# Grouped-query decode attention on one core: fewer instructions on VectorE and GpSimd

## The chip, the core and the metric

The kernel runs on one core of a Trainium2 chip. The metric is device time in microseconds (us) of one execution, taken as the median of ten runs. The engines are named as in the profile: PE is TensorE (matmul), PEld its weight load, DVE is VectorE, ACT is ScalarE, POOL is GpSimd, SP is SyncE, which here only issues transfers. Sixteen DMA engines move data between HBM and the core's memory (SBUF).

## The reference

One attention block with a key/value cache: 32 sequences of 4 new tokens, 32 query heads on 4 key/value heads of width 128, 2048 cached positions.

```python
B, Sq, D = 32, 4, 1024
Hq, Hkv, Sk, Dh = 32, 4, 2048, 128
...
q = (x @ wq).reshape(B, Sq, Hq, Dh)            # per head
scores = jnp.einsum("bhqd,bhkd->bhqk", q, k) * (Dh ** -0.5)
p = _softmax(scores, axis=-1)
o = jnp.einsum("bhqk,bhkd->bhqd", p, v)
return o.transpose(0, 2, 1, 3).reshape(B, Sq, Hq * Dh) @ wo
```

All arrays are bfloat16. K and V are 2 MB each per sequence, so 64 tiles of 2 MB, wq and wo are 8 MB each.

## The kernel before, in words

The program is written by hand, engine by engine. `_Program` collects each engine's operations in the order in which they are recorded and turns their dependences into semaphore waits. There is no scheduler: the order in the source is the order on the engine. On GpSimd every operation also waits for the one before it (`last_pool`).

**Transfers.** SP issues all loads in one fixed list: x, four pieces of wq, the first three K tiles, then V and K tiles in turn (line 189 on), then wo in eleven pieces (line 216 on). A tile of 2 MB has 128 rows of 16 KB, one per partition. The big buffer has eight slots: four for V, three for K, and one that GpSimd uses for masked probabilities. A K load waits until K of three sequences before was turned (`kt`, line 205), a V load until the product with V of four sequences before is done (`pv`, line 203). The wo pieces go into the slots of the last three K tiles and of V 28.

**One step** (line 436 on) handles sequence i up to its softmax, and sequence i-3 (LAG) with V:

- `kt(i+1)` (line 317): VectorE turns K in blocks of 32x32 as 32-bit words, in four chunks of 128x1024. Two chunks stand ahead of the max of step i, two behind it.
- `qd(i+1)` (line 307): GpSimd copies q of one sequence into a block-diagonal buffer, four copies of 32x64, one for each key/value head. A token `t_qd` is given to PE.
- `pe_qk(i)` (line 325): 16 matmuls write 128 x 2048 scores. PE takes `t_kt`, `t_qd` and `t_exp`.
- `softmax_max` (line 344): a max over the scores on VectorE, and a second small operation that multiplies it by -scale.
- `softmax_exp` (line 349): ScalarE computes exp(scale * s + bias) and the row sums.
- `pe_sum`, `recip` (lines 361, 365): a matmul with one column gathers the sums, VectorE takes their reciprocal.
- `pt(i)` (line 356): VectorE turns the probabilities; two buffers.
- `pd(i-1)` (line 371): GpSimd spreads them into a block-diagonal buffer, four copies of 32x1024; a token `t_pd` is given to PE. For the last two sequences VectorE does some of them.
- `pe_pv(i-3)` (line 381): 64 matmuls with V. `o_evac` (line 393): ScalarE scales by the reciprocal and writes o over that sequence's q.
- `o_turn` (line 399): VectorE turns o for the output projection, four sequences at a time from step 22 on; the rest behind the loop (line 468).

**The end.** `oproj` (line 409) runs 64 matmuls, two for each head, in the order of the wo pieces (4, 4, 4, 4, 4, 4, 2, 2, 2, 1, 1 heads). `oproj_out` copies the result and stores it.

PE's program has a run-time loop over four steps at a time; all other engines' programs are straight code.

Of the kernel before, what the change touches and what calls it, by code (L numbers as in the profile page):

```python
# [29 lines left out]
class _Program:  # L30
# [14 lines left out]

    def op(self, engine, emit, waits=(), done=None, takes=(), gives=None):
        if engine == "pool":
            done = done or ("pool", self.count["pool"])
            waits = tuple(waits) + (self.last_pool,) * (self.last_pool is not None)
            self.last_pool = done  # L50
        if gives is not None:
            self.late[engine].append(done)
        elif done is not None:
            self.count[engine] += 1
            for d in [done] + self.late[engine]:
                assert d not in self.at, d
                self.at[d] = (engine, self.count[engine])
            self.late[engine] = []
        self.ops[engine].append((emit, tuple(waits), tuple(takes), (gives or engine, 1) if done is not None else None))
# [44 lines left out]
def bass_standalone__gqa_block_cached__sampling_kernel(  # L104
# [17 lines left out]
    TC = 16  # L122
    NCH = T // TC
    KT = D // 128
    NS = 8
# [5 lines left out]
    KS = 3  # L131
    LAG = 3
    QB = 4
    NC = D // 2
# [7 lines left out]
    with ExitStack() as es:  # L142
# [6 lines left out]
        q_sb = KT_sb[:, 1, :, :, :, :].rearrange("p t a r w -> p (t a r w)")[:, 0:Hq * Dh]  # L149
        q_sb = q_sb.rearrange("p (h a g e) -> p h a g e", h=REP, a=2, g=G)  # L150
        QT_sb = sbuf("QT_sb", [128, B, 2, REP, Sq, 2], BF16)
        oT_sb = sbuf("oT_sb", [128, Hq // 4, 2, B, Sq, 2], BF16)
        QD_sb = sbuf("QD_sb", [128, 2, 2, G, 32, 2], BF16)
# [3 lines left out]
        xT_sb = P_flat[:, D:2 * D].rearrange("p (a b) -> p a b", b=128)  # L157
        PT_sb = sbuf("PT_sb", [128, 2, T // 2, 32, 2], BF16)
        PD_sb = sbuf("PD_sb", [128, T // 2, 4, G, 8, 2], BF16)
# [4 lines left out]
        permf = sbuf("permf", [128, 128], F32)  # L164
        mx = sbuf("mx", [128, 4], F32)
        negmx = sbuf("negmx", [128, 4], F32)
# [32 lines left out]
        for kind, b in loads:  # L199
            s = slot_of(kind, b)  # L200
            waits = ["qproj"] * (b < VS) if kind == "v" else []
            if kind == "v" and b >= VS:
                waits = [("pv", b - VS)]
            if kind == "k" and b >= KS:
                waits = [("kt", b - KS, NCH - 1)]
            src = (k_cache if kind == "k" else v_cache)[b].rearrange("g (r t) d -> (g r) t d", r=R)
            p.dma("sp", lambda e, s=s, src=src: e.dma_start(big[:, s, :, :], src), waits, (kind, b), f"s_b{s}", kind == "v")
# [8 lines left out]
        for c, m in enumerate(WO):  # L216
            assert u0 // 4 == (u0 + m - 1) // 4
            kind, b = wo_for[u0 // 8]
            dst, src = wo_at(u0, m), wo_v[:, u0 // 4, u0 % 4 * D:(u0 % 4 + m) * D]
            p.dma("sp", lambda e, dst=dst, src=src: e.dma_start(dst, src),  # L220
                [("kt", b, NCH - 1) if kind == "k" else ("pv", b)], ("wo", c), f"s_wo{c}")
            u0 += m
# [46 lines left out]
        for n, j in enumerate(QJ):  # L269
            g, y = j // 2, j % 2  # L270
            dst = q_sb.rearrange("p (x y) a g e -> p x y a g e", y=2)[:, :, y, :, g, :]
            src = ps_q(j).rearrange("p (h a e) -> p h a e", h=4, a=2)
            if n % 2 == 0:
                p.op("dve", lambda e, s=src, d=dst: e.tensor_copy(d, s), [q_of(j)], ("qs", j))  # L274
            else:
                p.op("act", lambda e, s=src, d=dst: e.activation(d, s, ACT.Copy), [q_of(j)], ("qs", j))

# [29 lines left out]
        def qd(i):  # L307
            for g in range(G):
                rows = slice(32 * g, 32 * (g + 1))
                src = words(QT_sb[rows, i, :, :, :, :].rearrange("p a h s w -> p a (h s w)"))  # L310
                dst = words(QD_sb[rows, i % 2, :, g, :, :].rearrange("p a q w -> p a (q w)"))
                waits = ["qd0"] + [("qa", 3, 1)] + [("qb", 3, 1)] * (i >= QB) + ([("qk", i - 2)] if i > 1 else [])
                p.op("pool", lambda e, s=src, d=dst: e.tensor_copy(d, s), waits if g == 0 else [],  # L313
                     ("qd", i) if g == G - 1 else None)
            p.give("pool", ("qd", i), "t_qd")

        def kt(i, chunks):
            for c in chunks:
                ts = slice(TC * c, TC * (c + 1))
                src = words(big[:, slot_of("k", i), ts, :].rearrange("p t d -> p (t d)"))  # L320
                dst = words(KT_sb[:, i % 2, ts, :, :, :].rearrange("p t a r w -> p (t a r w)"))
                waits = [("k", i)] + ([("qk", i - 2)] if i > 1 else ["qt_all"] if i == 1 else [])
                p.op("dve", lambda e, s=src, d=dst: e.transpose(d, s), waits, ("kt", i, c), gives="t_kt" if c == NCH - 1 else None)  # L323

        def pe_qk(i):
            waits = [] if i else [("qs", j) for j in range(8)]
            takes = [("t_kt", 1), ("t_qd", 1)] + [("t_exp", 1)] * (i > 0)
            for a in range(2):
# [15 lines left out]
        def softmax_max(i):  # L344
            p.op("dve", lambda e: e.tensor_reduce(mx[:, i % 4:i % 4 + 1], ps_s[:, :], AX.X, ALU.max), [("qk", i)], ("mx", i))  # L345
            p.op("dve", lambda e: e.tensor_scalar(negmx[:, i % 4:i % 4 + 1], mx[:, i % 4:i % 4 + 1], -scale, None, op0=ALU.mult),  # L346
                 [("mx", i)], ("negmx", i))

        def softmax_exp(i):
            p.op("act", lambda e: e.activation(  # L350
                P_sb[:, :, :, :].rearrange("p t r w -> p t w r"), ps_s[:, :].rearrange("p (t w r) -> p t w r", w=2, r=R),
                ACT.Exp, bias=negmx[:, i % 4:i % 4 + 1], scale=scale, accum_out=ssum[:, i % 4:i % 4 + 1]),
                [("negmx", i)] + ([("pt", i - 1)] if i else ["qproj"]), ("exp", i))
            p.give("act", ("exp", i), "t_exp")

        def pt(i):
            src = words(P_flat)
            dst = words(PT_sb[:, i % 2, :, :, :].rearrange("p t q w -> p (t q w)"))
            p.op("dve", lambda e: e.transpose(dst, src), [("exp", i)] + ([("pd", i - 2, G - 1)] if i > 1 else []), ("pt", i))  # L359

        def pe_sum(i):
            p.op("pe", lambda e: e.matmul(ring[i % 4][:, 511:512], lhsT=permf[:, :], rhs=ssum[:, i % 4:i % 4 + 1], start=True, stop=True),  # L362
                 ["permf"] if i == 0 else [], ("ss", i), [("t_exp", 1)] * (i == L))

        def recip(i):
            p.op("dve", lambda e: e.reciprocal(rinv[:, i % 4:i % 4 + 1], ring[i % 4][:, 511:512]), [("ss", i)], ("rinv", i))

# [3 lines left out]
        def pd(i):  # L371
            free = ("pv", i - 2) if i > 1 else ("pd0", "pf0")[i]
            for g in range(G):
                rows = slice(32 * g, 32 * (g + 1))
                src = words(PT_sb[rows, i % 2, :, :, :].rearrange("p t (x q) w -> p (t x) (q w)", x=4))
                dst = words(pd_of(i)[rows, :, :, g, :, :].rearrange("p t x q w -> p (t x) (q w)"))
                p.op("dve" if i >= B - 2 and g < i - B + 4 else "pool", lambda e, s=src, d=dst: e.tensor_copy(d, s), [("pt", i), free], ("pd", i, g))  # L377
            if i < B - 2:
                p.give("pool", ("pd", i, G - 1), "t_pd")

        def pe_pv(i, t):
            takes, waits = [], []
            if t == 0:
                ring_of["o", i] = slot()
                takes = [("t_pd", 1)] * (i < B - 2) + [(f"s_b{slot_of('v', i)}", 16)]
                waits = [] if i < B - 2 else [("pd", i, g) for g in range(G)]
            buf = ring_of["o", i]
# [44 lines left out]
        qd(0)  # L432
        kt(0, range(NCH))
        starts = []
        idle_rhs = ident[:, :].unsqueeze(1).to_broadcast([128, IDLE // 128, 128])
        for i in range(B + LAG):
            j = i - LAG
            starts.append(len(p.ops["pe"]))
            if i < L:
                qd(i + 1)  # L440
                kt(i + 1, (0, 1))
            if i < B:
# [4 lines left out]
            if i < B:  # L447
                pe_idle(20 if i < LAG else 5, ring[j % 4][:, 0:IDLE], idle_rhs, [("qb", 3, 1), ("qs", 3)] if i == 0 else [])
                softmax_exp(i)
            if 0 < i < B:  # L450
                recip(i - 1)
            if i < L:
                kt(i + 1, (2, 3))
            if 21 < i and 4 * (i - 22) + 4 <= i - LAG:
                o_turn(4 * (i - 22), 4)
            if i < B:
# [9 lines left out]
            if 0 < i <= B:  # L466
                pd(i - 1)
        for b0, n in ((24, 4), (28, 2), (30, 1), (31, 1)):
            o_turn(b0, n)
# [4 lines left out]
        p.loop = starts[4:B + 1:4]  # L474
        names = list(p.ENGINES) + ["t_kt", "t_qd", "t_exp", "t_pd", "t_o"] + sorted({s for s in p.dma_count})
        sems = {n: es.enter_context(nc.semaphore(f"e_{n}" if n in p.ENGINES else n)) for n in names}
# [53 lines left out]
```

## Time and profile before

| what | value |
|---|---|
| time, median of 10 runs (lowest to highest) | 364.65 us (364.5 to 364.85) |
| the profiled execution: time, span | 364.57 us, 362.8 us |
| PE busy | 309.0 us, 85% |
| DVE busy, instructions | 279.1 us, 77%, 295 |
| ACT busy | 102.8 us, 28% |
| POOL busy, instructions | 165.4 us, 46%, 262 |
| granted PE clock | 0.995 |
| HBM read | 151.26 MB |

The span is from the first to the last instruction of the profile; 1.77 us of the execution lie around it. Idle time of an engine that is not the bound costs nothing. The groups of VectorE and GpSimd that the change touches (columns: line, engine, operation, out<-in, shapes, count | busy us, mean ns of one | idle before in us and what ended it):

```profile
L323 DVE STREAM_TRANSPOSE KT_sb<-big 128x1024 f32<-128x1024 f32 x128 | 150.1, 1212 | 7.8 <-DMA big<-in_k_cache_dram 7.8
...
L359 DVE STREAM_TRANSPOSE PT_sb<-P_sb 128x1024 f32<-128x1024 f32 x32 | 39.8, 1245 | 10.9 <-ACT P_sb L350 10.9
L366 DVE RECIPROCAL rinv<-ps_r 128x1 f32<-128x1 f32 x32 | 5.1, 158 | 0.2 <-PE ps_r L362 0.2
L346 DVE TENSOR_SCALAR negmx<-mx 128x1 f32<-128x1 f32 x32 | 4.9, 154 | 1.1
L404 DVE STREAM_TRANSPOSE oT_sb<-QT_sb 128x128 f32<-128x128 f32 x14 | 3.3, 273 | 0.0
```

GpSimd's copies are 123 of 1034 ns (`pd`) and 128 of 229 ns (`qd`).

### The profile page before, as it was taken

The page shows a single profiled execution, that of the slowest core. Times are in us where ns is not written, and L with a number is a line of the kernel's source. Part 1 is how long each engine was busy: PE and PEld are TensorE (multiplying, and loading weights), DVE is VectorE, ACT ScalarE, POOL GpSimd, SP SyncE. Part 2 cuts the span into 40 slices and gives each one's busy share as a digit, 9 for nine tenths or more (in the row PEclk, how much of TensorE's full clock was granted, in tenths as well). Part 3 has the DMA queues.
Part 4 walks back from the last instruction along what each step waited for, and adds up shares of the span by engine and source line. Part 5 has one row for each costly group of instructions (what it writes and reads, how often), then busy time and mean ns, then how long its engine had stood idle before and what let it go on. Part 6 is the DMA issues. An engine that isn't in the chain of part 4 may idle for free. (4 is left out here: it accounts for less than half of the span.)

```text
span 362.8 us, 6454 instructions
## 1 busy us (share of the span) xinstructions
PE 309.0 (85%) x3002; PEld 147.3 (41%) x2338; DVE 279.1 (77%) x295; ACT 102.8 (28%) x110; POOL 165.4 (46%) x262
## 2 busy tenths in 40 slices
PE   1988787999999999999999999888888888889796
PEld 1002000444444444444444444444433334449611
DVE  0028779999999999999999999899888888856300
ACT  1014222333333333333333333332332223333000
POOL 8002155055555555555555555444555555443000
PEclk9999989999999999999999999999999999999999
DMA  7999999999999999999999999999999999999994
GB/s 323 430 432 434 434 434 417 423 428 430 428 426 425 425 434 428 430 429 425 426 429 430 431 428 423 428 430 430 430 426 423 430 433 430 428 425 424 417 413 159
DMA packets 11822, 151.69 MB, mean 418 GB/s; under 512 B 1312, under 2 KB 1568, under 8 KB 2336
## 3 DMA queue, kind: packets, MB, share of 16 engines
q1 hardware_dynamic: 11664, 151.39, 98.4%
q8 instruction: 6, 0.10, 0.1%
q10 hardware_dynamic: 144, 0.13, 0.1%
q14 instruction: 8, 0.07, 0.0%
HBM read 151.26 MB, written 0.26 MB: 418 GB/s over the span
## 5 line engine op out<-in xcount | busy, mean ns | idle before, releaser
L323 DVE STREAM_TRANSPOSE KT_sb<-big 128x1024 f32<-128x1024 f32 x128 | 150.1, 1212 | 7.8 <-DMA big<-in_k_cache_dram 7.8
L350 ACT ACTIVATE P_sb<-ps_s,negmx 128x2048 bf16<-128x2048 f32 x32 | 82.0, 2564 | 191.2 <-DVE negmx L346 191.2
L16 PE MATMUL ps_s<-KT_sb,QD_sb 128*128 128x512 bf16 x384 | 105.0, 381 | 0.0
L377 POOL COPY PD_sb<-PT_sb 32x1024 f32<-32x1024 f32 x62 | 64.1, 1034 | 70.3 <-PE ps_r L388 45.4
L377 POOL COPY big<-PT_sb 32x1024 f32<-32x1024 f32 x61 | 63.1, 1034 | 61.2 <-PE ps_r L388 36.6
L345 DVE TENSOR_REDUCE mx<-ps_s 128x1 f32<-128x2048 f32 x32 | 73.3, 2292 | 14.3 <-PE ps_s L16 13.5
L388 PE MATMUL ps_r<-big 128*128 128x128 bf16 x1024 | 59.8, 219 | 9.7 <-PEq L85 9.5
L336 PE MATMUL ps_s<-KT_sb,QD_sb 128*128 128x512 bf16 x128 | 48.8, 381 | 21.8 <-PEq L85 21.8
L388 PE MATMUL ps_r<-big,PD_sb 128*128 128x128 bf16 x1024 | 59.8, 219 | 7.6 <-PEq L85 7.5
L388 PEld LDWEIGHTS ps_r<-big 128*128 128x128 bf16 x1024 | 58.0, 98 | 20.2 <-issue 19.7
L388 PEld LDWEIGHTS ps_r<-big,PD_sb 128*128 128x128 bf16 x1024 | 58.1, 98 | 18.4 <-issue 17.6
L336 PEld LDWEIGHTS ps_s<-KT_sb,QD_sb 128*128 128x128 bf16 x128 | 12.4, 97 | 108.4 <-issue 108.4
L359 DVE STREAM_TRANSPOSE PT_sb<-P_sb 128x1024 f32<-128x1024 f32 x32 | 39.8, 1245 | 10.9 <-ACT P_sb L350 10.9
L313 POOL COPY QD_sb<-QT_sb 32x64 f32<-32x64 f32 x128 | 29.4, 229 | 37.4 <-DVE QT_sb L292 20.3
L16 PE MATMUL ps_r<-ident 128*128 128x384 bf16 x173 | 33.3, 325 | 0.0
L362 PEld LDWEIGHTS ps_r<-ssum,permf 128*128 128x128 f32 x64 | 11.9, 187 | 24.8 <-issue 23.1
L397 ACT ACTIVATE QT_sb<-ps_r,rinv 128x128 bf16<-128x128 f32 x32 | 11.8, 367 | 24.5 <-PE ps_r L388 22.0
L274 DVE CAST KT_sb<-ps_r 128x512 bf16<-128x512 f32 x2 | 1.3, 687 | 20.1 <-PE ps_r L258 20.1
L414 PE MATMUL ps_s<-big,oT_sb 128*128 128x512 bf16 x32 | 12.2, 380 | 2.2 <-DMA big<-in_wo_dram 1.3
L423 DVE CAST P_sb<-ps_s 128x512 bf16<-128x512 f32 x1 | 0.7, 692 | 16.0 <-PE ps_s L16 16.0
L16 PE MATMUL ps_s<-big,oT_sb 128*128 128x512 bf16 x32 | 12.1, 379 | 0.0
L247 PE MATMUL ps_r<-ident 128*128 128x384 bf16 x32 | 10.3, 323 | 0.0
(42 smaller groups left out, 93.9 us busy)
## 6 DMA issues: line engine op xcount, KB each, us to landing
big<-in_k_cache_dram SPq DMA_DIRECT2D x32, 2048.0 KB, 15.4
big<-in_v_cache_dram SPq DMA_DIRECT2D x32, 2048.0 KB, 19.6
big<-in_wq_dram SPq DMA_DIRECT2D x4, 2048.0 KB, 13.9
big<-in_wo_dram SPq DMA_DIRECT2D x6, 1024.0 KB, 23.6
big<-in_wo_dram SPq DMA_DIRECT2D x3, 512.0 KB, 25.1
big<-in_wo_dram SPq DMA_DIRECT2D x2, 256.0 KB, 21.0
P_sb<-in_x_dram SPq DMA_DIRECT2D x1, 256.0 KB, 2.7
out_dram<-P_sb ACTq DMA_DIRECT2D x1, 128.0 KB, 1.8
```

What stands on the lines that cost most here:

```text
L16: return eng.add_instruction(mybir.InstMatmult(name=nc.get_next_instruction_name(), engine=eng.engine, start_tensor_calc=start, stop_tenso ...
L313: p.op("pool", lambda e, s=src, d=dst: e.tensor_copy(d, s), waits if g == 0 else [], ("qd", i) if g == G - 1 else None)
L323: p.op("dve", lambda e, s=src, d=dst: e.transpose(d, s), waits, ("kt", i, c), gives="t_kt" if c == NCH - 1 else None)
L336: mm = lambda e, a_=(out_, lhsT, rhs), f=first, l=last: e.matmul(a_[0], lhsT=a_[1], rhs=a_[2], start=f, stop=l, skip_group_check=True)
L345: p.op("dve", lambda e: e.tensor_reduce(mx[:, i % 4:i % 4 + 1], ps_s[:, :], AX.X, ALU.max), [("qk", i)], ("mx", i))
L350: p.op("act", lambda e: e.activation(P_sb[:, :, :, :].rearrange("p t r w -> p t w r"), ps_s[:, :].rearrange("p (t w r) -> p t w r", w=2, r=R),
L359: p.op("dve", lambda e: e.transpose(dst, src), [("exp", i)] + ([("pd", i - 2, G - 1)] if i > 1 else []), ("pt", i))
L362: p.op("pe", lambda e: e.matmul(ring[i % 4][:, 511:512], lhsT=permf[:, :], rhs=ssum[:, i % 4:i % 4 + 1], start=True, stop=True), ["permf"] ...
L377: p.op("dve" if i >= B - 2 and g < i - B + 4 else "pool", lambda e, s=src, d=dst: e.tensor_copy(d, s), [("pt", i), free], ("pd", i, g))
L388: p.op("pe", lambda e: e.matmul(buf[:, 0:Dh], lhsT=pd_of(i)[:, t // 2, :, :, :, t % 2].rearrange("p x g q -> p (x g q)"), rhs=big[:, slot_ ...
L397: p.op("act", lambda e: e.activation(dst, src, ACT.Copy, scale=rinv[:, i % 4:i % 4 + 1]), [("pv", i), ("rinv", i)], ("o", i))
L414: mm = lambda e, a=(out_, lhsT, rhs), h=h: e.matmul(a[0], lhsT=a[1], rhs=a[2], start=(h == 0), stop=(h == Hq - 1), skip_group_check=True)
```

## The change

- K is turned in two operations of 128x2048 a sequence in place of four of 128x1024; one stands where each pair stood.
- q is multiplied by the scale when it is copied out of PSUM, so the exponential has no scale, and the max is negated by the reduction itself; the small operation behind it goes.
- The row sums of two sequences lie in neighbouring columns, and one reciprocal takes both.
- GpSimd gives PE one token a step (`t_pool`), after `qd`, in place of two. `qd` is recorded two sequences ahead, behind `pd`. Its second copy waits for `pt` of two sequences before; the copies within `pd` and `qd` no longer wait for each other. `pt` has three buffers in place of two and no longer waits for `pd`.
- o of sequences 0 to 29 is turned in one go (two operations of 128x960) behind the loop. Its target lies over the first half of the turned K.

```diff
-            waits = tuple(waits) + (self.last_pool,) * (self.last_pool is not None)
+            waits = tuple(waits) + (self.last_pool,) * (chain and self.last_pool is not None)
...
-                waits = [("kt", b - KS, NCH - 1)]
+                waits = [("kt", b - KS, 1)]
...
-                p.op("dve", lambda e, s=src, d=dst: e.tensor_copy(d, s), [q_of(j)], ("qs", j))
+                p.op("dve", lambda e, s=src, d=dst: e.tensor_scalar(d, s, scale, None, op0=ALU.mult), [q_of(j)], ("qs", j))
...
-                p.op("pool", lambda e, s=src, d=dst: e.tensor_copy(d, s), waits if g == 0 else [],
-                     ("qd", i) if g == G - 1 else None)
-            p.give("pool", ("qd", i), "t_qd")
+                p.op("pool", lambda e, s=src, d=dst: e.tensor_copy(d, s), waits if g == 0 else [("pt", i - 2)] * (g == 1 and i > 1),
+                     ("qd", i) if g == G - 1 else None, chain=g == 0)
+            p.give("pool", ("qd", i), "t_pool")
...
-                ts = slice(TC * c, TC * (c + 1))
+                ts = slice(KC * c, KC * (c + 1))
...
-            p.op("dve", lambda e: e.tensor_reduce(mx[:, i % 4:i % 4 + 1], ps_s[:, :], AX.X, ALU.max), [("qk", i)], ("mx", i))
-            p.op("dve", lambda e: e.tensor_scalar(negmx[:, i % 4:i % 4 + 1], mx[:, i % 4:i % 4 + 1], -scale, None, op0=ALU.mult),
-                 [("mx", i)], ("negmx", i))
+            p.op("dve", lambda e: e.tensor_reduce(
+                negmx[:, i % 4:i % 4 + 1], ps_s[:, :], AX.X, ALU.max, negate=True), [("qk", i)], ("negmx", i))
...
-            p.op("dve", lambda e: e.transpose(dst, src), [("exp", i)] + ([("pd", i - 2, G - 1)] if i > 1 else []), ("pt", i))
+            p.op("dve", lambda e: e.transpose(dst, src), [("exp", i)], ("pt", i))
...
-            p.op("dve", lambda e: e.reciprocal(rinv[:, i % 4:i % 4 + 1], ring[i % 4][:, 511:512]), [("ss", i)], ("rinv", i))
+            n = 1 if i >= L - 1 else 2
+            src = ring[i % 4][:, 510 + i % 2:510 + i % 2 + n]
+            p.op("dve", lambda e: e.reciprocal(rinv[:, i % 4:i % 4 + n], src), [("ss", i + n - 1)], ("rinv", i))
...
-            if i < B - 2:
-                p.give("pool", ("pd", i, G - 1), "t_pd")
...
-                takes = [("t_pd", 1)] * (i < B - 2) + [(f"s_b{slot_of('v', i)}", 16)]
+                takes = [(f"s_b{slot_of('v', i)}", 16)]
...
-                qd(i + 1)
-                kt(i + 1, (0, 1))
+                kt(i + 1, (0,))
...
-                kt(i + 1, (2, 3))
-            if 21 < i and 4 * (i - 22) + 4 <= i - LAG:
-                o_turn(4 * (i - 22), 4)
+                kt(i + 1, (1,))
...
+            if i + 2 < B:
+                qd(i + 2)
-        for b0, n in ((24, 4), (28, 2), (30, 1), (31, 1)):
+        for b0, n in ((0, 30), (30, 1), (31, 1)):
```

More of the change, by code (lines that the diff above doesn't have):

```diff
@@ L44, in __init__, with op @@
         self.loop = None
-    def op(self, engine, emit, waits=(), done=None, takes=(), gives=None):
+    def op(self, engine, emit, waits=(), done=None, takes=(), gives=None, chain=True):
         if engine == "pool":
             done = done or ("pool", self.count["pool"])
-            waits = tuple(waits) + (self.last_pool,) * (self.last_pool is not None)
+            waits = tuple(waits) + (self.last_pool,) * (chain and self.last_pool is not None)
             self.last_pool = done
@@ L123, in bass_standalone__gqa_block_cached__sampling_kernel @@
     NCH = T // TC
+    KC = T // 2
     KT = D // 128
@@ L132, in bass_standalone__gqa_block_cached__sampling_kernel @@
     LAG = 3
+    PB = 3
     QB = 4
@@ L150, in bass_standalone__gqa_block_cached__sampling_kernel @@
         q_sb = q_sb.rearrange("p (h a g e) -> p h a g e", h=REP, a=2, g=G)
+        oT_sb = KT_sb[:, 0, :, :, :, :].rearrange("p t a r w -> p (t a r w)")[:, 0:Hq * NT].rearrange(
+            "p (h a b s w) -> p h a b s w", h=Hq // 4, a=2, b=B, s=Sq)
         QT_sb = sbuf("QT_sb", [128, B, 2, REP, Sq, 2], BF16)
-        oT_sb = sbuf("oT_sb", [128, Hq // 4, 2, B, Sq, 2], BF16)
         QD_sb = sbuf("QD_sb", [128, 2, 2, G, 32, 2], BF16)
@@ L157, in bass_standalone__gqa_block_cached__sampling_kernel @@
         xT_sb = P_flat[:, D:2 * D].rearrange("p (a b) -> p a b", b=128)
-        PT_sb = sbuf("PT_sb", [128, 2, T // 2, 32, 2], BF16)
+        PT_sb = sbuf("PT_sb", [128, PB, T // 2, 32, 2], BF16)
         PD_sb = sbuf("PD_sb", [128, T // 2, 4, G, 8, 2], BF16)
@@ L164, in bass_standalone__gqa_block_cached__sampling_kernel @@
         permf = sbuf("permf", [128, 128], F32)
-        mx = sbuf("mx", [128, 4], F32)
         negmx = sbuf("negmx", [128, 4], F32)
@@ L220, in bass_standalone__gqa_block_cached__sampling_kernel @@
             p.dma("sp", lambda e, dst=dst, src=src: e.dma_start(dst, src),
-                [("kt", b, NCH - 1) if kind == "k" else ("pv", b)], ("wo", c), f"s_wo{c}")
+                [("kt", b, 1) if kind == "k" else ("pv", b)], ("wo", c), f"s_wo{c}")
             u0 += m
@@ L273, in bass_standalone__gqa_block_cached__sampling_kernel @@
             if n % 2 == 0:
-                p.op("dve", lambda e, s=src, d=dst: e.tensor_copy(d, s), [q_of(j)], ("qs", j))
+                p.op("dve", lambda e, s=src, d=dst: e.tensor_scalar(d, s, scale, None, op0=ALU.mult), [q_of(j)], ("qs", j))
             else:
-                p.op("act", lambda e, s=src, d=dst: e.activation(d, s, ACT.Copy), [q_of(j)], ("qs", j))
+                p.op("act", lambda e, s=src, d=dst: e.activation(d, s, ACT.Copy, scale=scale), [q_of(j)], ("qs", j))
         xT_flat = xT_sb.rearrange("p a b -> p (a b)")
@@ L322, in kt @@
                 waits = [("k", i)] + ([("qk", i - 2)] if i > 1 else ["qt_all"] if i == 1 else [])
-                p.op("dve", lambda e, s=src, d=dst: e.transpose(d, s), waits, ("kt", i, c), gives="t_kt" if c == NCH - 1 else None)
+                p.op("dve", lambda e, s=src, d=dst: e.transpose(d, s), waits, ("kt", i, c), gives="t_kt" if c else None)
         def pe_qk(i):
             waits = [] if i else [("qs", j) for j in range(8)]
-            takes = [("t_kt", 1), ("t_qd", 1)] + [("t_exp", 1)] * (i > 0)
+            takes = [("t_kt", 1), ("t_pool", 1)] + [("t_exp", 1)] * (i > 0)
             for a in range(2):
@@ L351, in softmax_exp @@
                 P_sb[:, :, :, :].rearrange("p t r w -> p t w r"), ps_s[:, :].rearrange("p (t w r) -> p t w r", w=2, r=R),
-                ACT.Exp, bias=negmx[:, i % 4:i % 4 + 1], scale=scale, accum_out=ssum[:, i % 4:i % 4 + 1]),
+                ACT.Exp, bias=negmx[:, i % 4:i % 4 + 1], accum_out=ssum[:, i % 4:i % 4 + 1]),
                 [("negmx", i)] + ([("pt", i - 1)] if i else ["qproj"]), ("exp", i))
@@ L357, in pt @@
             src = words(P_flat)
-            dst = words(PT_sb[:, i % 2, :, :, :].rearrange("p t q w -> p (t q w)"))
-            p.op("dve", lambda e: e.transpose(dst, src), [("exp", i)] + ([("pd", i - 2, G - 1)] if i > 1 else []), ("pt", i))
+            dst = words(PT_sb[:, i % PB, :, :, :].rearrange("p t q w -> p (t q w)"))
+            p.op("dve", lambda e: e.transpose(dst, src), [("exp", i)], ("pt", i))
         def pe_sum(i):
-            p.op("pe", lambda e: e.matmul(ring[i % 4][:, 511:512], lhsT=permf[:, :], rhs=ssum[:, i % 4:i % 4 + 1], start=True, stop=True),
+            p.op("pe", lambda e: e.matmul(ring[(i if i == L else i // 2 * 2) % 4][:, 510 + i % 2:511 + i % 2], lhsT=permf[:, :], rhs=ssum[:, i % 4:i % 4 + 1], start=True, stop=True),
                  ["permf"] if i == 0 else [], ("ss", i), [("t_exp", 1)] * (i == L))
         def recip(i):
-            p.op("dve", lambda e: e.reciprocal(rinv[:, i % 4:i % 4 + 1], ring[i % 4][:, 511:512]), [("ss", i)], ("rinv", i))
+            n = 1 if i >= L - 1 else 2
+            src = ring[i % 4][:, 510 + i % 2:510 + i % 2 + n]
+            p.op("dve", lambda e: e.reciprocal(rinv[:, i % 4:i % 4 + n], src), [("ss", i + n - 1)], ("rinv", i))
+            if n == 2:
+                p.at["rinv", i + 1] = p.at["rinv", i]
         def pd_of(i):
@@ L374, in pd @@
                 rows = slice(32 * g, 32 * (g + 1))
-                src = words(PT_sb[rows, i % 2, :, :, :].rearrange("p t (x q) w -> p (t x) (q w)", x=4))
+                src = words(PT_sb[rows, i % PB, :, :, :].rearrange("p t (x q) w -> p (t x) (q w)", x=4))
                 dst = words(pd_of(i)[rows, :, :, g, :, :].rearrange("p t x q w -> p (t x) (q w)"))
-                p.op("dve" if i >= B - 2 and g < i - B + 4 else "pool", lambda e, s=src, d=dst: e.tensor_copy(d, s), [("pt", i), free], ("pd", i, g))
-            if i < B - 2:
-                p.give("pool", ("pd", i, G - 1), "t_pd")
+                p.op("dve" if i >= B - 2 and g < i - B + 4 else "pool", lambda e, s=src, d=dst: e.tensor_copy(d, s), [free] * (g == 0 or i >= B - 2) + [("pt", i)] * (i >= B - LAG), ("pd", i, g), chain=g == 0 or i >= B - 2)
         def pe_pv(i, t):
@@ L384, in pe_pv @@
                 ring_of["o", i] = slot()
-                takes = [("t_pd", 1)] * (i < B - 2) + [(f"s_b{slot_of('v', i)}", 16)]
-                waits = [] if i < B - 2 else [("pd", i, g) for g in range(G)]
+                takes = [(f"s_b{slot_of('v', i)}", 16)]
+                waits = [] if i < B - LAG else [("pd", i, g) for g in range(G)]
             buf = ring_of["o", i]
@@ L432, in bass_standalone__gqa_block_cached__sampling_kernel @@
         qd(0)
-        kt(0, range(NCH))
+        qd(1)
+        kt(0, (0, 1))
         starts = []
@@ L449, in bass_standalone__gqa_block_cached__sampling_kernel @@
                 softmax_exp(i)
-            if 0 < i < B:
-                recip(i - 1)
+            if 0 < i < B and i % 2 == 0:
+                recip(i - 2)
+            if i == L:
+                recip(L - 1)
             if i < L:
-                kt(i + 1, (2, 3))
-            if 21 < i and 4 * (i - 22) + 4 <= i - LAG:
-                o_turn(4 * (i - 22), 4)
+                kt(i + 1, (1,))
             if i < B:
@@ L474, in bass_standalone__gqa_block_cached__sampling_kernel @@
         p.loop = starts[4:B + 1:4]
-        names = list(p.ENGINES) + ["t_kt", "t_qd", "t_exp", "t_pd", "t_o"] + sorted({s for s in p.dma_count})
+        names = list(p.ENGINES) + ["t_kt", "t_pool", "t_exp"] + sorted({s for s in p.dma_count})
         sems = {n: es.enter_context(nc.semaphore(f"e_{n}" if n in p.ENGINES else n)) for n in names}
```

## The prediction

> **What bounds the kernel now.** I read the slice rows first, then the queue's own waits, the stage windows, the chain that ended last, and the completion marks of the transfers. The slice rows and the queue table of the page:
>
> ```profile
> DVE  0028779999999999999999999899888888856300
> ...
> DMA  7999999999999999999999999999999999999994
> GB/s 323 430 432 434 434 434 417 423 428 430 428 426 425 425 434 428 430 429 425 426 429 430 431 428 423 428 430 430 430 426 423 430 433 430 428 425 424 417 413 159
> ...
> q1 hardware_dynamic: 11664, 151.39, 98.4%
> q8 instruction: 6, 0.10, 0.1%
> ...
> q14 instruction: 8, 0.07, 0.0%
> HBM read 151.26 MB, written 0.26 MB: 418 GB/s over the span
> ```
>
> The reader is to see that the 16 DMA engines are full from the first slice to the last but one, at the same rate where VectorE has 9 as where it has 2. A packet of 16 KB takes 614 ns in the trace (median of 8710), so 16 engines give 16 x 16384 / 614 = 427 GB/s: that is the row. No slice shows an empty queue. The queue's waits and the windows of the end (columns: window, its length, PE, PEld, DVE, ACT, POOL busy, clock, DMA share, GB/s):
>
> ```profile
> SPq L207 <- DVE PT_sb L359: 169.0, 22, 9.8
> ...
> 355.00:356.00 1.00, 1.00 (x6) 0.20 (x2) 0.00 (x0) 0.00 (x0) 0.00 (x0) 1.00 0.88 340
> 356.00:357.00 1.00, 1.00 (x6) 0.29 (x3) 0.00 (x0) 0.00 (x0) 0.00 (x0) 1.00 0.58 223
> 357.00:358.00 1.00, 0.85 (x5) 0.10 (x1) 0.00 (x0) 0.00 (x0) 0.00 (x0) 1.00 0.21 80
> 358.00:359.00 1.00, 1.00 (x6) 0.20 (x2) 0.00 (x0) 0.00 (x0) 0.00 (x0) 1.00 0.04 14
> ```
>
> SP waits a step at a time for a buffer, but with several transfers outstanding: a 2 MB tile lands 15 to 20 us after its issue and takes only 4.9 us of the engines. So these waits cost nothing. The windows show how the stream ends: not at once, but with the share falling from 0.88 over 0.58 to 0.21. Some engines are done at 356 us, others three microseconds later. The chain ends on the last of them:
>
> ```profile
> 332.68 25.12 DMA big<-in_wo_dram
> 357.80 0.05 issue
> 357.84 0.39 PE ps_s L414
> ```
>
> After it come eight matmuls for four heads, the copy and the store (to 362.8). PE is not the bound there: it starts the projection at 343.89, 64 matmuls at 0.216 take 13.8, and its gaps for wo chunks sum to some 2 us.
>
> **Why the engines end apart.** Each transfer leaves 16 completion marks in the trace, one per DMA engine. Their distances from the first mark, in us, for a tile before any code was fetched, one in mid-run, and the last wo chunk:
>
> ```
>  57.05: 0 .05 .06 .14 .15 .16 .17 .18 .20 .21 .22 .24 .25 .26 .27 .33
> 292.06: 0 .01 .03 .04 .06 .09 .11 .14 .26 .66 1.47 1.52 1.61 1.70 1.79 2.02
> 356.14: 0 .06 .08 .12 .15 .18 .65 1.10 1.43 1.51 1.51 1.57 1.66 1.75 2.13 2.94
> ```
>
> The marks jump when an engine's sequencer fetches code, and stay. Six fetches of 16 KB (q8: 58.0, 76.3, 89.6, 103.3, 335.6, 344.3) each threw another engine back by about 1.5. The fetches of 8 KB (q14) at 84.4, 187.8 and 296.8 came when GpSimd had executed 71, 198 and 324 instructions, and moved one and the same engine to .88, 1.53 and 2.17. Those at 82.3, 208.2 and 332.2 came at 61, 188 and 312 instructions of VectorE, and moved one engine to 1.0, 2.03 and 3.0. Two more (157.0, 335.9) fit ScalarE and SP. So 8 KB hold some 127 instructions, and the engine that ends last is VectorE's fetcher, 2.94 behind; next GpSimd's, 2.13; then TensorE's six, at most 1.75.
>
> **Parts of the change, against the profiled execution (364.57, its span 362.8; the median of the runs is 0.08 higher).**
>
> K in two ops. 128 of 1212 ns become 64 of 2048 words. From 273 ns (128x128) to 1212 (128x1024) a word costs 939/896 = 1.048 ns, so one takes 2.285; the pair now takes 2.35 start to end. That saves 0.065, twice a step; the ends are 0 (2.35) and 0.15 (twice the 1.048 without any fixed part is 2.15, and half of that is got at most). The Trainium skill, "VectorE: DVE Perf Modes", section on the errata of SBUF-source ops, says each instruction pays a fixed extra, with about 150 cycles measured: 64 fewer would give 64 x 0.156 = 10 us of VectorE, by the rows 64 x 0.065 = 4.2. I take the rows. In either case it lies beside transfers: nothing at the end.
>
> Max negated. 32 x 154 ns = 4.9 us busy go, and they stand between max and exponential. From 60 to 235 us the kernel runs steps of 8.97 (max at 76.13, 85.10, 94.07) by the chain scores, max, exponential; those become some 8.85. The stream needs 9.8 per step (4.19 MB at 427 GB/s), so compute catches up sooner and then waits: nothing. Reciprocals in pairs, 15 x 158 ns: the same cover.
>
> q scaled. Four VectorE casts (687) and four ScalarE copies (594 to 610) keep shape and source; a multiplication in place of a copy is not shown; between -0.1 and +0.3 each, and I take 0 by those rows. The cover is what is queued: the third K load is still 2 us and V0 7 us from landing when K3 is issued at 35.85.
>
> One token. The order on GpSimd stays qd, pd, qd, pd; but three of four QD copies now wait for the turned P (pt) of two steps before, and pd is queued behind them. In the trace pd(29) starts at 312.92, directly after pt; it becomes 3 x 0.27 later. Its reader, pv(29), runs at 330.38: 12 us of cover; QD itself is done at 313.8 and read at 322.4. Were this gone, V buffers would come late by that 0.8 per step. pt waits no more for pd; its row shows no such wait.
>
> o in one go. Twelve turns of 273 ns leave the loop. Two of 128x960 (273 + 832 x 1.048 = 1145) come at the end, in place of four that took 0.76 at 337.30. They end at 339.6, o(30)'s at 339.9; the last turn waits until 343.44 for pv(31): 3.5 us of cover. If a turn were wholly proportional (7.5 x 273 = 2.05) it still fits. oT over K's first half waits for nothing new: qk(30) read it by 316.1.
>
> SP issues the same transfers in the same order; the K loads wait for the second of two ops, the same point.
>
> Code. Counted in the two programs with waits and branches, VectorE goes from 331 to 177 instructions, GpSimd from 367 to 310, TensorE 960 to 954, ScalarE and SP stay. With fetches near 61, 189, 317 VectorE keeps one of three, and GpSimd (71, 198, 325) two of three. Here a rule speaks against any gain: the Trainium skill, "Runtime: NRT & Kernel Launch", section "Instruction fetch mechanics", has code refilled in 16 KiB blocks while the page before executes, and a crossing "mostly hidden". By it this is worth 0, and the time stays 364.65. The rows agree that no engine waits for code, but the price appears on the DMA engine that carries it, and for one that lasts. I take the rows. VectorE's fetcher then ends at 1.0, GpSimd's at 1.5, and the last is one of TensorE's at 1.75: 2.94 - 1.75 = 1.19 earlier. The V31 tile lands earlier likewise (its spread was 3.04), so pv(31) and the projection start earlier, and PE's 2 us of gaps remain. Sum: 364.57 - 1.19 = 363.38, on the scale of the median 363.5.
>
> **Rivals.**
> - One fetch fewer only: the second of VectorE still comes before the stream's end (177 is 12 short of 189), or GpSimd's third does. Then 2.03 or 2.13 is last: 364.65 - 0.85 = 363.8. For it: the counts are read to within five instructions. Chance 0.08.
> - No change, 364.6: a lag that goes is replaced, for instance a TensorE fetch falls on GpSimd's engine (1.5 + 1.5 = 3.0). For it: 427 GB/s is untouched and all else is hidden. Against it: in before no two sequencers shared an engine. Chance 0.15.
> - Slower: the turn of o in one go ends after pv(31). The projection may start up to 2 us after its present 343.89 less the 1.2 gained, so the two turns may take 344.6 - 0.75 - 337.3 = 6.55; from 3.3 us each on they decide, and from 4.3 each the kernel is slower beyond the bound. At 5 us each it would be 337.3 + 10 + 0.75 + 13.8 = 361.9 for the last matmul in place of 359.8: 366.8. Against it: 273 ns for 128 words. With other late waits 0.07.
>
> **Numbers.** The forecast, 363.5, has 0.70 (363.0 to 363.9: the last of TensorE's lags between 1.43 and 2.0, and a little for the packing of the tail). The range 362.9 to 364.75 takes in both lesser outcomes; it leaves out the slower case. A measurement tells 0.2%, 0.73 us, from no change. Faster: 0.70 + 0.08, less 0.01 at the edge; same 0.15 plus that edge; slower 0.07.
>
> **What would show it.** Right: q14 has five packets of code, the spread of the last chunk's marks is under 2, DMA stays near 427 GB/s, the share in the end falls within 2 us, VectorE is busy some 265 us and steps before 200 us take under 8.9. Wrong: eight packets, or five with the spread still near 3; a gap in DMA; a projection that starts on the turn of heads rather than on pv(31).

## The result and the profile after

| | median us | lowest to highest |
|---|---|---|
| before | 364.68 | 364.5 to 365.29 (28 runs) |
| changed | 363.40 | 363.27 to 363.51 (8 runs) |

The ratio is 0.9964, with a 95% interval of 0.9955 to 0.9973: the changed kernel is 1.28 us faster, 0.35%. The forecast was 363.5.

The first profile of the changed kernel fell on a disturbed execution of 365.15 us (one DMA engine was 1.9 us late from the first wq tile on; why is not known), so the second profile, of the same kernel at 363.35 us with a span of 361.6, is shown here. First the slice rows and the queue table of its page:

```profile
DVE  0018799999898898879998888888888888856500
...
DMA  8999999999999999999999999999999999999995
...
q8 instruction: 6, 0.10, 0.1%
...
q14 instruction: 5, 0.04, 0.0%
HBM read 151.26 MB, written 0.26 MB: 419 GB/s over the span
```

VectorE is busy for 269.1 us in place of 279.1; GpSimd is as busy as before (165.3 for 165.4), only its program is shorter. The stream of 151 MB is as full as it was. In the table of the queues the packets of one row differ: q14, the queue with the code of VectorE, GpSimd, ScalarE and SP, has five in place of eight. Now the stage windows of the end (window, length, then busy time of PE, PEld, DVE, ACT, POOL; clock, DMA share, GB/s) and the chain that ended last (start, duration, what):

```profile
355.00:356.00 1.00, 0.95 (x5) 0.19 (x2) 0.00 (x0) 0.00 (x0) 0.00 (x0) 1.00 0.92 354
356.00:357.00 1.00, 0.79 (x4) 0.19 (x2) 0.00 (x0) 0.00 (x0) 0.00 (x0) 1.00 0.58 221
357.00:358.00 1.00, 1.00 (x7) 0.20 (x2) 0.00 (x0) 0.00 (x0) 0.00 (x0) 1.00 0.10 39
358.00:359.00 1.00, 0.53 (x3) 0.00 (x0) 0.43 (x1) 0.60 (x1) 0.00 (x0) 1.00 0.00 0
```

```profile
332.10 24.48 DMA big<-in_wo_dram
356.58 0.05 issue
356.63 0.39 PE ps_s L417
```

The reader is to see that the stream begins to thin out at the same time, with 0.58 between 356 and 357 us as before, but is over by 358 us, where it lasted until just past 359. The wo piece on which the chain ends lands at 356.58 in place of 357.80. What follows it is the same eight matmuls, copy and store. This piece is the third from the end. The last piece lands 1.27 us after it in both kernels, with nearly the same spread, before its own two matmuls are due; so its marks measure the end, though the end does not wait for them. They are, in us from the first mark, before and after:

```
before, first at 356.14:  0 .06 .08 .12 .15 .18 .65 1.10 1.43 1.51 1.51 1.57 1.66 1.75 2.13 2.94
after,  first at 355.97:  0 .18 .32 .35 .40 .41 .98 1.28 1.30 1.52 1.57 1.76 1.78 1.84 1.86 1.88
```

The trace names no engine at a mark or a packet; which engine is meant is read here and below from the jumps of the marks behind each fetch. The first engine ends 0.17 us earlier than before. VectorE's fetcher, which was the last, has come forward, and the last is now one of the six that carried TensorE's code.

### The profile page after: what moved, and what is told of

It reads as the page before. It is cut to its first block, busy times and chain, and to the rows that moved or that the text cites. A ratio compares the mean times of both kernels' runs of the same rounds, so it can differ in the third digit from the quotient of the medians.

```text
span 363.4 us, 6213 instructions
## 1 busy us (share of the span) xinstructions
PE 307.5 (85%) x3002; PEld 146.8 (40%) x2338; DVE 269.1 (74%) x170; ACT 102.8 (28%) x110; POOL 165.3 (46%) x262
## 5 line engine op out<-in xcount | busy, mean ns | idle before, releaser
L325 DVE STREAM_TRANSPOSE KT_sb<-big 128x2048 f32<-128x2048 f32 x64 | 146.6, 2293 | 16.6 <-DMA big<-in_k_cache_dram 16.6
L16 PE MATMUL ps_s<-KT_sb,QD_sb 128*128 128x512 bf16 x384 | 103.7, 377 | 0.0
L347 DVE TENSOR_REDUCE negmx<-ps_s 128x1 f32<-128x2048 f32 x32 | 73.2, 2287 | 12.6 <-PE ps_s L16 11.3
L338 PE MATMUL ps_s<-KT_sb,QD_sb 128*128 128x512 bf16 x128 | 48.3, 377 | 18.3 <-PEq L85 18.3
L276 DVE TENSOR_SCALAR KT_sb<-ps_r 128x512 bf16<-128x512 f32 x2 | 1.3, 686 | 21.6 <-PE ps_r L260 21.6
L417 PE MATMUL ps_s<-big,KT_sb 128*128 128x512 bf16 x32 | 12.2, 380 | 2.2 <-DMA big<-in_wo_dram 1.2
L16 PE MATMUL ps_s<-big,KT_sb 128*128 128x512 bf16 x32 | 12.1, 379 | 0.0
```

The lines of the kernel that those rows point to most:

```text
L16: return eng.add_instruction(mybir.InstMatmult(name=nc.get_next_instruction_name(), engine=eng.engine, start_tensor_calc=start, stop_tenso ...
L338: mm = lambda e, a_=(out_, lhsT, rhs), f=first, l=last: e.matmul(a_[0], lhsT=a_[1], rhs=a_[2], start=f, stop=l, skip_group_check=True)
L347: p.op("dve", lambda e: e.tensor_reduce(negmx[:, i % 4:i % 4 + 1], ps_s[:, :], AX.X, ALU.max, negate=True), [("qk", i)], ("negmx", i))
L417: mm = lambda e, a=(out_, lhsT, rhs), h=h: e.matmul(a[0], lhsT=a[1], rhs=a[2], start=(h == 0), stop=(h == Hq - 1), skip_group_check=True)
```

## The experiments

Each was timed beside the kernel before, on the same chip. The number of instructions counts waits and branches.

**The changed kernel once more**, without an edit.

> The changed kernel once more, unaltered, for a second profile. Fetch theory (the end is the DMA engine with the most code fetches): 363.4 us; in the profile two fetches on GpSimd's DMA engine, one on VectorE's, five of 8 KB in all, and the last wo chunk's marks spread over 1.7 to 2.0 us, the last of them on an engine that carried 16 KB of TensorE's code. Rival (the late engine of the first profile of this kernel, 1.9 us late from the first wq tile on and 3.5 in the end, is how this kernel always runs): a spread of about 3.5 again and a span of 363.4 against 361.6.

Measured: 363.45 us, ratio 0.9967 (0.9955 to 0.9979). Five packets of 8 KB, a spread of 1.88, and the last mark on an engine set back by TensorE's code. The late engine of the first profile is not the kernel's way: there TensorE's second fetch fell on the engine that was 1.9 late already, and it ended 3.55 behind.

**Code given back to VectorE, no work in the steps.** The copies run while VectorE waits for wq.

```diff
+        for n in range(160):
+            p.op("dve", lambda e, n=n: e.tensor_copy(junk[:, n:n + 1], identf[:, 0:1]), ["identf"] if n == 0 else [])
```

> The changed kernel with 160 copies of 128x1 on VectorE into a spare tile, while it waits for wq between 5 and 25 us; 177 instructions become 337, no step is touched. Fetch theory: three 8 KB fetches by VectorE again (near its instructions 61, 189, 317), its DMA engine ends about 3.0 behind the first in place of 1.0, so 1.2 us of the gain are given back: 364.6 us. Rival (the gain came from VectorE's shorter steps, or from the earlier waits): nothing in the steps changes, so 363.4 us.

> As the one with 160, with 290 copies: 467 instructions. Fetch theory: four fetches by VectorE, its DMA engine about 4.0 behind, 363.4 + 2.2 = 365.6 us, slower than the kernel before. Rival: 363.4 us, or a little more if the copies reach past 25 us and hold up the scaling of q.

Measured: 364.54 us with 160 copies, ratio 0.9999 (0.9991 to 1.0007), and 365.55 with 290, ratio 1.0027 (1.0016 to 1.0038): slower than the kernel before. The timeline of the first shows where the copies stand (start, duration, what), and its stage windows show the end:

```profile
5.18 9.76 DVE L248 COPY junk<-identf 128x1 f32<-128x1 f32 x160
26.02 1.29 DVE L279 TENSOR_SCALAR KT_sb<-ps_r 128x512 bf16<-128x512 f32 x2 [11.08 <-PE ps_r L263]
```

```profile
356.00:357.00 1.00, 0.95 (x5) 0.24 (x3) 0.00 (x0) 0.00 (x0) 0.00 (x0) 1.00 0.58 225
357.00:358.00 1.00, 0.84 (x4) 0.10 (x1) 0.00 (x0) 0.00 (x0) 0.00 (x0) 1.00 0.17 64
358.00:359.00 1.00, 1.00 (x6) 0.20 (x2) 0.00 (x0) 0.00 (x0) 0.00 (x0) 1.00 0.03 12
```

The copies are over by 15 us, and VectorE then idles for 11 us as it would have anyway. All later work is that of the changed kernel. Yet the third microsecond of the tail is back, 0.03 of the engines between 358 and 359: half an engine's time. VectorE's fetches come at 10.9, 35.0 and 297.8 us. The last four marks of six tiles, two around each fetch:

```
  8.12: ...  .28  .29  .42  .51
 13.01: ...  .30  .41  .50 1.02
 32.59: ...  .30  .42  .51 1.03
 37.48: ...  .29  .41  .50 2.00
292.01: ... 1.68 1.80 2.01 2.05
296.89: ... 1.69 1.85 2.06 2.98
```

One engine steps to 1.0, 2.0 and 3.0. The third step comes some 280 us after the last copy, so it is not the copies' own work that sets the engine back. With 290 copies there are four fetches, and it ends 3.92 behind. So the whole gain and more goes back on code alone. The first 160 copies bring two more fetches and cost 1.1 us, since the first of the two brings the engine to 2.0 only, little beyond the 1.88 that TensorE's code leaves anyway; the one more that the kernel with 290 has costs 1.0. The rival, that shorter steps or fewer waits are what gains, falls. This kernel with 160 also answers another question: GpSimd's code is as short in it as in the changed kernel (310), and it is no faster than the kernel before. GpSimd's saving alone is worth nothing while VectorE's fetcher is last.

**Code given back to GpSimd.** As above, with 180 memsets of one column.

```diff
+        for n in range(180):
+            p.op("pool", lambda e, n=n: e.memset(junk[:, n:n + 1], 0.0), [], chain=False)
```

> The changed kernel with 180 memsets of 128x1 on GpSimd into a spare tile, in its idle time between 10 and 30 us; 310 instructions become 490. Fetch theory: four fetches by GpSimd (near 71, 199, 327, 455) in place of two, its DMA engine about 0.88 + 3 x 0.65 = 2.8 behind in place of 1.5: last by about 1.0 over TensorE's 1.75, so 364.4 us. Rival (GpSimd's and VectorE's instruction count as such is free): 363.4 us.

Measured: 364.28 us, ratio 0.9989 (0.9983 to 0.9996), and in its profiled execution (364.58) a spread of 2.88 at the end, on the engine that four fetches set back. That engine had begun some 0.5 late, which may be why this execution lies above the median. GpSimd's code costs time too, then, as soon as the engine that carries it is the last.

**One part of the change alone, on the kernel before.** K in two operations; then q scaled when made and the max negated.

```diff
-                ts = slice(TC * c, TC * (c + 1))
+                ts = slice(KC * c, KC * (c + 1))
```

> The kernel before with K in two operations alone: VectorE 267 instructions, GpSimd's 367 as before. Fetch theory: VectorE's third fetch is gone (267 is under 317), its DMA engine ends near 2.0, and GpSimd's with three fetches near 2.15 is last: 0.8 less than the kernel before, 363.8 to 363.9 us. Rival (the gain goes with VectorE's busy time, 10 us in the whole change): K in two ops has 4 of these 10, so 0.5 of the gain of 1.2, 364.15 us.

```diff
-            p.op("dve", lambda e: e.tensor_scalar(negmx[:, i % 4:i % 4 + 1], mx[:, i % 4:i % 4 + 1], -scale, None, op0=ALU.mult),
-                 [("mx", i)], ("negmx", i))
```

> The kernel before with q scaled when made and the max negated by the reduction, nothing else: VectorE 300 instructions, 32 fewer than 331 and 64 for K untouched. Fetch theory: 300 is under 317 too, so the third fetch goes here as well, and this small edit gives as much as K in two ops: 363.8 to 363.9 us. Rival (gain in proportion to instructions removed, 154 in the whole change): 31 of 154 of 1.2 is 0.25, so 364.4 us.

Measured: 363.76 and 363.69 us, both with the ratio 0.9974 (0.9964 to 0.9985). Sixty-four instructions and thirty-one give the same, because each takes VectorE's count below the third fetch: both have seven packets in q14, two of them VectorE's. A gain in proportion to busy time (364.15 for K) or to instructions (364.4 for the max) is outside what was measured. The last marks lie 2.35 behind the first (with K alone, on VectorE's engine, which began 0.5 late) and 2.12 (with the max alone). With K alone GpSimd's had been expected to be the last; VectorE's is the last in both, with the max alone by 0.06 only.

**Code given to TensorE.**

```diff
+        pe_idle(256, ring[0][:, 0:16], ident[:, 0:16])
```

> The changed kernel with 256 small matmuls on TensorE (128x16 into a bank that the projection overwrites), between 4.5 and about 14 us while it waits for wq: 16 KB more of its code. Fetch theory: one 16 KB fetch more; TensorE's fetches have each fallen on another DMA engine, so the seventh sets an engine back by 1.5 that has no lag, and nothing is later than the present last one: 363.4 us, with seven q8 packets. If it falls on an engine with a lag already, 1.5 to 1.0 + 1.5 = 2.5 to 3.0: up to 364.6. Rival (each fetch takes its bytes from the whole stream): 16 KB at 427 GB/s is 0.04 us: no change either, but then the fetches of VectorE couldn't have cost 1.1 us.

Measured: 363.52 us, ratio 0.9968 (0.9956 to 0.998). There are seven q8 packets, the additional one at 12.3 us; the marks show it on an engine that no other fetch had set back, and the spread at the end is 1.90. So twice the code of a VectorE fetch is free here: by the marks TensorE's blocks go to an engine of their own each time, while VectorE's and GpSimd's pile up on one engine each.

**All profiles in one table.** The last mark of the last wo piece, and the time of the same profiled execution:

| kernel | VectorE, GpSimd instructions | first mark | spread | last mark | time of this execution | time less last mark |
|---|---|---|---|---|---|---|
| before | 331, 367 | 356.14 | 2.94 | 359.07 | 364.57 | 5.50 |
| changed, second profile | 177, 310 | 355.97 | 1.88 | 357.85 | 363.35 | 5.50 |
| changed, first profile | 177, 310 | 356.10 | 3.55 | 359.65 | 365.15 | 5.50 |
| 160 copies | 337, 310 | 356.13 | 2.88 | 359.02 | 364.51 | 5.49 |
| 290 copies | 467, 310 | 356.12 | 3.92 | 360.04 | 365.55 | 5.51 |
| 180 memsets | 177, 490 | 356.21 | 2.88 | 359.09 | 364.58 | 5.49 |
| K alone | 267, 367 | 356.00 | 2.35 | 358.35 | 363.85 | 5.50 |
| max alone | 300, 367 | 356.07 | 2.12 | 358.20 | 363.70 | 5.50 |
| 256 matmuls | 177, 310 | 356.07 | 1.90 | 357.97 | 363.49 | 5.52 |

The first mark moves by 0.24 in all nine, the last by 2.2, and the time follows the last one to within 0.03. That is the whole account of the difference: 1.22 of the 1.22 us between the profiled executions of before and after.

## Why the prediction was right, step by step

- **The bound.** Right: 16 full DMA engines, and an end set by the slowest of them.
- **The fetches.** Right in number (one and two of three stay) and in effect. The lags were forecast at 1.0 for VectorE's engine, 1.5 for GpSimd's and 1.75 for the last of TensorE's; they are 1.28, 1.52 and 1.88. What was left out is that the engines already stood up to 0.4 apart before any fetch in this execution (0.33 in that of before). The gain was forecast as 1.19; it is 1.28 by the medians and 1.22 between the two profiled executions. That it came out so close is in part luck: of the 1.22, only 1.06 is the smaller spread; the rest is an earlier first mark, which no step of the prediction had. There was luck in the margin too: the first fetch in the changed kernel came at VectorE's instruction 47 and not 61, and in the kernel with 160 copies the next one came when 177 instructions of its trace had started. The changed kernel has 175 there, so by this count its second fetch would have come at the very end, behind the last transfer.
- **The rule and the row.** The "mostly hidden" of the Trainium skill ("Runtime: NRT & Kernel Launch", section "Instruction fetch mechanics") agrees with the engines' rows, which name no wait for code (what they call "issue" stays open). The experiments show that it doesn't hold for the transfers. By the rule the copies cost nothing; they cost 1.1 and 2.1 us over the changed kernel.
- **VectorE's operations.** The groups of the second profile (by shape; line, engine, operation, out<-in, count | busy us, mean ns | idle before):

```profile
L325 DVE STREAM_TRANSPOSE KT_sb<-big 128x2048 f32<-128x2048 f32 x64 | 146.6, 2293 | 16.7 <-DMA big<-in_k_cache_dram 16.7
...
L369 DVE RECIPROCAL rinv<-ps_r 128x2 f32<-128x2 f32 x15 | 2.4, 158 | 0.0
...
L407 DVE STREAM_TRANSPOSE KT_sb<-QT_sb 128x960 f32<-128x960 f32 x2 | 2.2, 1156 | 0.0
```

  The operation on K takes 2293 ns (2285 was worked out), the turn of o 1156 (1145). The 64 operations fewer on K free 3.5 us of VectorE (150.1 to 146.6): near the 4.2 that the prediction took from the rows, far from the 10 of a fixed extra for each instruction. Scaling q takes 684 and 678 where the cast took 687 and 682: the unknown was zero. The idle time before K grew from 7.8 to 16.7 us, always for K's transfer: most of what VectorE gains, it waits there. Its busy time is 269.1 us where "some 265" was said; that figure was too low even by its own terms (279.1 less 4.2, 4.9 and 2.4 is 267.6).
- **The steps.** They were to take some 8.85 us before 200 us. The timeline of VectorE:

```profile
64.81 2.29 DVE L347 TENSOR_REDUCE negmx<-ps_s 128x1 f32<-128x2048 f32 x1 [0.39 <-PE ps_s L16]
...
73.60 2.29 DVE L347 TENSOR_REDUCE negmx<-ps_s 128x1 f32<-128x2048 f32 x1 [0.38 <-PE ps_s L16]
```

  They take 8.79, and a transfer of K first holds up these steps near 98 us; the stream's end shows nothing of the time gained there.
- **The token.** The cost was zero as forecast, but the reading behind it was wrong. The copy that starts at 312.92 before is pd(28), not pd(29), and it was not released by the turned P: pv(26), which frees its buffer, ended 0.15 earlier, and pt only happened to end at that moment too. In the changed kernel, pd starts on the product with V and QD follows at once (GpSimd's timeline):

```profile
312.41 4.31 POOL L382 COPY PD_sb<-PT_sb 32x1024 f32<-32x1024 f32 x4 [4.33 <-PE ps_r L391]
316.78 1.09 POOL L315 COPY QD_sb<-QT_sb 32x64 f32<-32x64 f32 x4
```

  The turned P that QD now waits for was ready before. So the 0.8 us of delay that the prediction allowed for does not show, and its cover was not needed. This term came out right by luck.
- **The rivals.** The turn of o in one go, with that of o(30) behind it, ended at 339.2 in the second profile, ahead of the last turn at 342.15 by 2.9 us: no cost. The projection starts at about 342.6 in place of 343.89 (its first matmul is not in the trace; the second starts at 342.81), on the turn that follows pv(31). The rival with one fetch fewer (363.8) is what the two kernels with one part each show: 363.76 and 363.69.

## What to carry to other kernels

When the DMA engines are full all the time, ask which of the sixteen ends last, and what else it carried: the completion marks of one transfer show it, the mean share does not. Instructions that cost an engine nothing can cost the transfers something, in steps: here one step for each 8 KB of straight code on VectorE or GpSimd, some 127 instructions. So removing 31 was worth as much as removing 64, and the 57 removed on GpSimd were worth nothing while VectorE's fetcher was last. Look for the next block's edge before shortening code for time.

## What the runs showed of the hardware that was not expected

- A DMA engine that is set back stays so: with the queue always full, the lag of 2.0 us that VectorE's engine got at 35 us in the kernel with 160 copies is still between 2.01 and 2.05 at 292 us.
- A fetch costs more than its packet. Code packets of 16 KB take 1.0 to 1.1 us and set their engine back by some 1.5; those of 8 KB take 0.31 (GpSimd) and 0.33 us (VectorE) and cost about 0.65 and 1.0. Why it is twice and three times the packet was not tried.
- By the marks, the sequencers' code shares the data's engines unevenly: all of VectorE's fetches on one engine and GpSimd's on one, TensorE's seven on seven. How the engine is chosen was not tried; no kernel here got rid of TensorE's lags of 1.5, which now set the end.
